# Every product of a transformer block as two 64-row halves that belong to different output tiles

## The chip, the cores and the metric

The kernel runs on one core of a Trainium2 chip. Time is device microseconds of that core for one execution, compared as medians of runs on the same chip. The engines of a core are TensorE (matrix products; in the trace PE, and PEld for its weight loads), VectorE (DVE), ScalarE (ACT), GpSimd (POOL) and SyncE (SP), whose queue issues nearly all DMAs. SBUF is the working memory with 128 partitions. PSUM, 8 banks of 2 KB a partition, is where products accumulate. [...]

## The reference

Sequence 2048, width D = 576, 32 heads of 18, feed-forward width 4608, everything float32:

```python
xn = _layernorm(x)
out = x + A(xn) + B(xn)
# A: qkv = xn @ wqkv (576 x 1728); every position attends to itself and to 7 earlier
#    ones, two apart (window 8, dilation 2); softmax over the 8; result @ wo (576 x 576)
# B: relu(xn @ w1) @ w2        (576 x 4608, 4608 x 576)
```

## The kernel before

**Tokens.** The even and the odd positions form two phases (`ph`), since a dilation of 2 never mixes them. A phase has 1024 tokens in 8 tiles of 128 (`i`), or 4 blocks of 256 (`tb`, two token tiles each).

**Precision.** Operands are split in a high part of type fp32r and a low part, so that a product of two float32 matrices is x_hi w_hi + x_lo w_hi + x_hi w_lo. D = 576 is four and a half times 128 rows. For the half, `mix` holds the 64 rows twice, their high part in partitions 0 to 63 and their low part in 64 to 127, and the weights hold the 64 rows twice. So `TERMS` (line 319) has 14 products of 128 rows: 4 + 4 with the high weights, one with `mix` and the high weights, 4 with the low weights, and one with `mix` and the low weights. That last one also computes low times low for the 64 rows, which the other rows do without.

**Slots.** Feed-forward columns are taken 128 at a time (36 groups, `c` in 12 chunks of C = 3 `f`). A slot `n` is one (ph, c, tb, f), 288 in all, `f` fastest, then `tb`; a chunk is 12 slots, a phase 144. In slot n the loop at line 765 emits, in this order and for all engines: `run_splits(n)`, the weight splits that are due; `h_mm(n + 2)`, the *first products* of a later slot (14 products of 256 columns into a bank `ph`), with their ReLU split into `hhi` (ScalarE) and `hlo` (VectorE); what is booked for the slot (`todo`: a qkv tile of 14 products of 432 columns into `pm`, transposes, wo products); `o_mm(n)`, the *second products* (two token tiles, two column cuts of 256 and 320, three terms: 12 products) into accumulators `po` that live through the three f of a token block; at f = 2 the adds of these to the residual `x` (line 613); `todo_late`; and `run_bg(margin)`, pieces of attention for VectorE as far as a count kept by the planner (`t["pe"]`, `t["dve"]`) stays within the margin, 3.0, 1.5 or 3.0 us by f. Each engine works through its own instructions strictly as emitted.

**Weights.** `split_task` queues them by step. A load is issued three tasks ahead of its split (`AHEAD`). The split (`two`, line 144) puts the high part on ScalarE and the low part on VectorE. Pools of C + 1 = 4 buffers hold w1 and w2. The step of w1 is s - 5 and that of w2 s - 3, where s is the first slot that uses it in second products (line 643).

**Attention.** A qkv unit (8 heads, 8 token tiles) starts every 26 slots from slot 7 of a phase. One tile is booked per slot, and then its attention goes to the background list.

**wo.** Each token tile's attention output is transposed by VectorE in 32-blocks and by a turn through DRAM (`wo_a`, `wo_f`), split (`wo_s`), multiplied (`wo_b`: 28 products into two `pm` banks) and added to `x`, spread over some 15 slots from 123 of a phase.

**PSUM.** Two tiles of two banks (`ps_o`), two banks for first products (`ps_h`), two for everything else (`ps_m`).

The opening (up to slot 7) is written out by hand. Between the phases, the second half of x is normed and transposed, in part by TensorE (lines 285 to 287) into `XT`.

## Time and profile before

| what | value |
|---|---|
| median of 3 runs | 1163.99 us (1163.91 to 1164.5) |
| the profiled execution, and its span | 1164.49 us, 1162.7 us |
| granted TensorE clock | 1.000 |
| TensorE busy / products | 1156.7 us / 8916 |
| VectorE busy | 822.3 us |
| ScalarE busy | 308.6 us |
| first products (`ph`) in the trace | 4018 |
| second products (`po`) | 2292 + 1146 |
| qkv products (`pm<-wq,xT`) | 896 |

How to read it: a matmul's busy time includes its run through the array, so the products overlap and a mean of 277 ns is not its price. The price is the distance between the starts of neighbours. "Idle before" of a group is how long its engine had stood still, and behind the arrow is what ended that. `ph`, `po`, `pm` are PSUM tiles; L113 is `mm`, the helper that all products go through, so that tiles and not lines tell them apart.

### The profile page before, as it was taken

Reading aid. Unit: us, or ns where it says so; the run is one execution under the profiler, and the core shown is the slowest. Engines: PE = TensorE matmul, PEld = TensorE weight load, DVE = VectorE, ACT = ScalarE, POOL = GpSimd, SP = SyncE. Lnnn points to the kernel's source line nnn. Section 1 sums busy time; section 2 is a strip of 40 time slices with the busy share of each in tenths; the row PEclk is TensorE's granted clock in tenths of the full one; section 3 lists DMA queues with packets and bytes.
Section 4 is the critical chain, followed back from the end, with each engine's and each line's share of the span. In section 5 each row is a group of like instructions: output and inputs, shape, how many; then the busy total and the mean of one; then the engine's idle time right before and its main releaser. Section 6 shows DMA issues by size and latency. Waiting matters only on the chain.

```text
span 1162.7 us, 21695 instructions
## 1 busy us (share of the span) xinstructions
PE 1156.7 (99%) x8916; PEld 1148.5 (99%) x8916; DVE 822.3 (71%) x1299; ACT 308.6 (27%) x748; POOL 44.8 (4%) x60
## 2 busy tenths in 40 slices
PE   9999999999999999999999999999999999999998
PEld 8999999999999999999999999999999999999998
DVE  7427885887687688876683288768868877887843
ACT  5322222131231221322433123222222312222210
POOL 2200100010000000000010001000100000000000
PEclk9999999999999999999999999999999999999999
DMA  5312211140321211365752113021312303113541
GB/s 184 98 32 79 69 48 54 39 112 1 94 79 32 81 39 46 96 156 112 180 164 69 43 53 95 22 81 38 87 35 61 110 1 101 46 32 95 123 100 63
DMA packets 149876, 88.66 MB, mean 76 GB/s; under 512 B 58528, under 2 KB 133536, under 8 KB 149776
## 3 DMA queue, kind: packets, MB, share of 16 engines
q1 hardware_dynamic: 146816, 78.61, 24.9%
q10 hardware_dynamic: 2960, 8.65, 2.5%
q8 instruction: 70, 1.15, 0.4%
q14 instruction: 30, 0.25, 0.1%
HBM read 67.90 MB, written 11.14 MB: 68 GB/s over the span
## 4 chain that ended last, share of the span: by engine, by line
PE 98%; SPq 1%; DMA 0%; DVE 0%; issue 0%; ACT 0%; DVEq 0%
PE ph L113 39%; PE po L113 38%; PE pm L113 20%; DMA st<-in_w 0%; PE pm L286 0%; SPq L162 0%; SPq L161 0%; DVE w2t L149 0%; SPq L157 0%; DVE x L619 0%; SPq L236 0%; PE pm L287 0%; DVE bst L250 0%; ACT w2t L145 0%; SPq L238 0%
## 5 line engine op out<-in xcount | busy, mean ns | idle before, releaser
L113 PE MATMUL ph<-xT,w1t 128*128 128x256 f32 x4018 | 504.9, 277 | 0.7 <-ACT xT L291 0.7
L113 PEld LDWEIGHTS ph<-xT,w1t 128*128 128x128 f32 x4018 | 486.7, 188 | 1.3 <-ACT xT L291 1.0
L113 PE MATMUL po<-w2t,hhi 128*128 128x256 f32 x2292 | 393.2, 293 | 0.2 <-DVE w2t L149 0.2
L113 PEld LDWEIGHTS po<-w2t,hhi 128*128 128x128 f32 x2292 | 335.4, 188 | 1.5 <-DVE w2t L149 0.4
L556 ACT ACTIVATE hhi<-ph 128x256 fp32r<-128x256 f32 x287 | 109.7, 383 | 582.3 <-PE ph L113 575.7
L113 PE MATMUL po<-w2t,hlo 128*128 128x256 f32 x1146 | 242.3, 292 | 0.0
L559 DVE SCALAR_TENSOR_TENSOR hlo<-ph,hhi 128x256 fp32r<-128x256 f32 x287 | 120.9, 421 | 164.7 <-ACT hhi L556 164.2
L113 PEld LDWEIGHTS po<-w2t,hlo 128*128 128x128 f32 x1146 | 188.9, 187 | 0.0
L113 PE MATMUL pm<-wq,xT 128*128 128x432 f32 x896 | 185.5, 358 | 0.0
L613 DVE TENSOR_TENSOR x<-po,x 128x576 f32<-128x576 f32 x190 | 143.0, 756 | 60.1 <-PE po L113 57.3
L113 PEld LDWEIGHTS pm<-wq,xT 128*128 128x128 f32 x896 | 163.8, 188 | 5.6
L421 DVE TENSOR_TENSOR pr<-qo,k 128x1152 f32<-128x1152 f32 x64 | 86.2, 1349 | 0.0
L424 DVE TENSOR_REDUCE lg<-pr 128x64 f32<-128x1152 f32 x64 | 85.1, 1343 | 0.0
L451 DVE TENSOR_TENSOR pr<-lg,v 128x1152 f32<-128x1152 f32 x64 | 84.7, 1349 | 0.0
L149 DVE TENSOR_TENSOR w2t<-st,w2t 128x576 fp32r<-128x576 f32 x72 | 55.8, 776 | 32.3 <-ACT w2t L145 32.2
L149 DVE TENSOR_TENSOR w1t<-st,w1t 128x640 fp32r<-128x640 f32 x70 | 58.8, 841 | 20.5 <-ACT w1t L145 20.4
L458 DVE TENSOR_TENSOR pr<-pr 128x288 f32<-128x288 f32 (+1 forms) x128 | 70.6, 600 | 0.0
L145 ACT ACTIVATE w2t<-st 128x576 fp32r<-128x576 f32 x72 | 49.3, 685 | 45.6 <-PE po L113 33.1
L390 ACT ACTIVATE k<-pm 128x144 f32<-128x144 f32 x64 | 18.6, 291 | 146.2 <-PE pm L113 146.2
L145 ACT ACTIVATE w1t<-st 128x640 fp32r<-128x640 f32 x72 | 52.9, 734 | 13.3 <-DMA st<-in_w 7.1
L427 POOL TENSOR_SCALAR_AFFINE_SELECT lg<-lg 1x512 f32<-1x512 f32 x8 | 9.9, 1232 | 809.7 <-DVE lg L424 705.8
L522 DVE TENSOR_TENSOR x<-pm,x 128x256 f32<-128x256 f32 (+1 forms) x32 | 13.2, 453 | 30.9 <-PE pm L113 30.9
(84 smaller groups left out, 470.8 us busy)
## 6 DMA issues: line engine op xcount, KB each, us to landing
st<-in_w SPq DMA_DIRECT2D x72, 288.0 KB, 3.1
st<-in_w SPq DMA_DIRECT2D x72, 256.0 KB, 3.2
st<-in_wqkv SPq DMA_DIRECT2D x32, 216.0 KB, 3.0
turned<-tr SPq DMA_DIRECT2D x64, 80.0 KB, 2.8
xn<-turned SPq DMA_DIRECT2D x16, 320.0 KB, 3.2
st<-in_w SPq DMA_DIRECT2D x144, 32.0 KB, 2.9
out<-x SPq DMA_DIRECT2D x15, 288.0 KB, 2.1
x<-in_x SPq DMA_DIRECT2D x14, 288.0 KB, 4.7
```

Source lines behind the costliest of these rows:

```text
L113: nc.tensor.matmul(o, l, r, start=start, stop=stop)
L145: nc.scalar.activation(hi, src, AF.Copy)
L149: nc.vector.tensor_tensor(lo, src, f32(hi), op=ALU.subtract)
L390: nc.scalar.activation(k[:, W - 1 + i, :], pq[:, 1, :], AF.Copy)
L421: nc.vector.tensor_tensor(pr[i], q, window(k, i), op=ALU.mult)
L424: nc.vector.tensor_reduce(lg[:, i], pr.pop(i).rearrange(heads, d=Dh), axis=AX.X, op=ALU.add)
L451: nc.vector.tensor_tensor(pr[i].rearrange(heads, d=Dh), e, window(v, i).rearrange(heads, d=Dh), op=ALU.mult)
L458: nc.vector.tensor_tensor(o, z[:, 0:n], z[:, n : 2 * n], op=ALU.add)
L522: nc.vector.tensor_tensor(acc, po[h], acc, op=ALU.add)
L556: nc.scalar.activation(hi, pt, AF.Relu)
L559: nc.vector.scalar_tensor_tensor(lo, pt, 0.0, f32(hi), op0=ALU.max, op1=ALU.subtract)
L613: nc.vector.tensor_tensor(acc, whole, acc, op=ALU.add)
```

## The change

Behind the opening, no product uses 128 rows any more. `mm_rows` issues two products of 64 rows each, one in partitions 0 to 63, one in 64 to 127, with different accumulators in different banks. Two output tiles are worked on together: in the first run tile A uses the lower rows and tile B the upper ones, in the second run they change places, and so each tile has both halves of the rows. Ahead of a run whose banks the other half of the rows has just written, a no-op on TensorE waits for the last product that did so.

The half tile of 64 rows is then a term of its own on either side: `LOWER` and `UPPER` have 13 pairs, `LOWER_MORE` and `UPPER_MORE` 14. For the upper side, `XT` has a tenth slice with a copy of the high part in partitions 64 to 127 (`twin`, `make_xt`, `xt_s`). Low times low of the 64 rows is not computed any more. Two tiles take 14 + 13 = 27 pairs.

First products (`h_two`): the pair of slots (g, g + 1), g = n + 2 for an even n, has its first run in slot n and its second in slot n + 1, where both ReLU splits follow. qkv (`qkv_tile`): two token tiles, first run in one slot, second in the next, then six copies. Second products (`o_two`): two token tiles, by column cut, four runs of three pairs. wo has no products of its own: its terms are appended to the second products of f = 1 in chunk 10, into the same accumulators. `ps_o` is four single banks, and the adds are four of one cut each. The steps of w1 and w2, the distance of qkv units (24) and the booking of wo's transposes are new. The `hp` pool has 3 buffers of each kind instead of 4.

```diff
+    def mm_rows(runs, behind=None):
+        if behind is not None:
+            tc.add_manual_dep(nc.tensor.nop().ins, behind.ins.name, SYNC, reason="PSUM banks change rows")
+        for pair in zip(*runs, strict=True):
+            for z, (o, l, r, start, stop, n) in zip((slice(0, 64), slice(64, P)), pair):
+                ins = nc.tensor.matmul(o, l[z], r[z], start=start, stop=stop)
+            t["pe"] += pair[0][5] / 2400.0 + 0.002
+        return ins
...
+    FULL_K = [(5 + k, k) for k in range(KT)] + [(k, k) for k in range(KT)] + [(5 + k, 5 + k) for k in range(KT)]
+    LOWER, LOWER_MORE = FULL_K + [(4, 4)], FULL_K + [(4, 4), (4, 9)]
+    UPPER, UPPER_MORE = FULL_K + [(4, 4)], FULL_K + [(4, 4), (9, 9)]
...
+        if not second:
+            for h in range(2):
+                PQ[h] = ps_m.tile([P, 3, UD], F32, name="pm")
+            PQ[2] = mm_rows((run(0, LOWER_MORE), run(1, UPPER_MORE)))
+            return
+        mm_rows((run(1, LOWER), run(0, UPPER)), PQ[2])
...
+    def h_two(g, second):
+        def run(n, terms):
+            ph, c, tb, f = slots[n]
+            w, xt = W1[ph, c, f], XT[ph, tb]
+            return [
+                (HP[n], w[:, b // 5, (b % 5) * P : (b % 5 + 1) * P], xt[:, a, :], not second and j == 0, second and j == len(terms) - 1, TBN)
+                for j, (a, b) in enumerate(terms)
+            ]
+        if not second:
+            HB["m"] = not HB["m"] and not busy_m.intersection((g - 3, g - 2, g - 1))
+            for n in (g, g + 1):
+                HP[n] = ps_m.tile([P, TBN], F32, name="pm") if HB["m"] else ps_h.tile([P, TBN], F32, name="ph")
+            HB["ins"] = mm_rows((run(g, LOWER_MORE), run(g + 1, UPPER_MORE)))
+            return
+        mm_rows((run(g + 1, LOWER), run(g, UPPER)), HB["ins"])
+        h_out(g)
+        h_out(g + 1)
...
+    def o_two(n):
+        ph, c, tb, f = slots[n]
+        hi, lo = H.pop(n)
+        w = W2[ph, c, f]
+        with_wo = c == WO_CHUNK and f == 1
+        if f == 0:
+            o_tiles(n)
...
+            z = [(l[:, cs], w[:, b, CUT[h]]) for l, b in ((hi, 0), (hi, 1), (lo, 0))]
+            if with_wo:
+                more = wo_run(ph, 2 * tb + k, h, (UPPER_MORE if upper else LOWER_MORE) if first else (UPPER if upper else LOWER), upper)
+                z = z + more
...
+        for j in range(4):
+            k, h = divmod(j, 2)
+            behind = PB[j - 2] if j > 1 else PB[3] if j == 0 and f else None
+            PB[j] = mm_rows((run(k, h, False), run(1 - k, h, True)), behind)
...
+        o_out(n, rows=True)
...
-                plan.append((HEADW[f] if first else s - 5, w1_task, ((ph, c, f), c * C + f)))
-                plan.append((HEADW[3 + f] if first else s - 3, w2_task, ((ph, c, f), c * C + f)))
+                plan.append((HEADW[f] if first else s + (-5, -4, -2)[f], w1_task, ((ph, c, f), c * C + f)))
+                plan.append((HEADW[3 + f] if first else s + (-3, -1, 0)[f], w2_task, ((ph, c, f), c * C + f)))
...
-        m = n + LAG
-        if m < len(slots):
-            h_mm(m)
+        g = n - n % 2 + LAG
+        if n < ROW0:
+            h_mm(n + LAG)
+        elif g < len(slots):
+            h_two(g, n % 2 == 1)
...
-        if n >= 0:
+        if ROW0 - 1 <= n < len(slots) - C:
+            o_two(n)
+        else:
             o_mm(n, n != HALVED)
```

The last three slots use the old `o_mm` with whole rows.

More of the change, by code (lines that the diff above doesn't have):

```diff
@@ L16 @@
 PSUM = bass.MemoryType.PSUM
+SYNC = mybir.DependencyInfo(mybir.DependencyClass.Sync, mybir.DependencyReason.DATA)
 P = 128
@@ L27 @@
 LAG = 2
+ROW0 = 8
 EPS = 1e-5
-UNIT0, UNIT_STEP, WO_AT = 7, 26, 12
+UNIT0, UNIT_STEP = 7, 24
+WO_CHUNK = 10
 XT_STEPS = (
@@ L37 @@
 )
-WO_STEPS = (0, 1, 3, 4, 6, 7, 9, 10)
+WO_STEPS = ((-5, -4), (-3, -3), (-1, -1))
 HEADW = (-9, -8, -7, -6, -5, -4)
@@ L83, in tile_body @@
     stp = pool("stp", 5)
-    hp = pool("hp", LAG + 2)
+    hp = pool("hp", LAG + 1)
     prp = pool("prp", 2)
@@ L89, in tile_body @@
     turned = pool("turned", 4, space=bass.MemoryType.DRAM)
-    ps_o = pool("ps_o", 2, space=PSUM)
+    ps_o = pool("ps_o", 4, space=PSUM)
     ps_h = pool("ps_h", 2, space=PSUM)
@@ L100, in tile_body @@
     spare = consts.tile([P, 1], F32, name="spare")
-    warm = ps_o.tile([P, 2, 512], F32, name="po")
+    warm = ps_o.tile([P, 512], F32, name="po")
     for _ in range(WARM):
-        nc.tensor.transpose(warm[:, 0, 0:P], ident, ident)
+        nc.tensor.transpose(warm[:, 0:P], ident, ident)
     x_v = x.rearrange("(p i two) d -> two i p d", i=NI, two=NPH)
@@ L278, in transpose_split @@
         if bank is ps_o:
-            po = ps_o.tile([P, 2, 512], F32, name="po")
-            pa, pb = po[:, 0, :].rearrange("p (k c) -> p k c", k=KT), po[0:DR, 1, 0:P]
+            pa = ps_o.tile([P, 512], F32, name="po").rearrange("p (k c) -> p k c", k=KT)
+            pb = ps_o.tile([P, 512], F32, name="po")[0:DR, 0:P]
         else:
@@ L312, in make_xt, with twin @@
         if h == 0:
-            XT[ph, tb] = xtp.tile([P, 9, TBN], F32R, name="xT")
+            XT[ph, tb] = xtp.tile([P, 10, TBN], F32R, name="xT")
         d = XT[ph, tb][:, :, h * P : (h + 1) * P]
         xn = XN.pop((ph, i))
-        return transpose_split(xn, d[:, 5:9, :], d[:, 4, :], d[:, 0:4, :], bank, parts)
+        steps = transpose_split(xn, d[:, 5:9, :], d[:, 4, :], d[:, 0:4, :], bank, parts)
+        if ph:
+            nc.scalar.activation(d[DR:P, 9, :], f32(d[0:DR, 4, :]), AF.Copy)
+        return steps
+    def twin(tb):
+        nc.scalar.activation(XT[0, tb][DR:P, 9, :], f32(XT[0, tb][0:DR, 4, :]), AF.Copy)
     TERMS = (
@@ L349, in xt_f @@
         if h == 0:
-            XT[ph, tb] = xtp.tile([P, 9, TBN], F32R, name="xT")
+            XT[ph, tb] = xtp.tile([P, 10, TBN], F32R, name="xT")
         z, td = f32(XT[ph, tb][:, 0:5, h * P : (h + 1) * P]), TD.pop((ph, i))
@@ L359, in xt_s @@
         d = XT[ph, tb][:, :, h * P : (h + 1) * P]
-        z = tmp.tile([P, 5, P], F32R, name="oT", bufs=1)[:, 0]
-        mix = d[:, 4, :]
+        mix, z = d[:, 4, :], d[:, 9, :]
         nc.scalar.activation(d[:, 5:9, :], f32(d[:, 0:4, :]), AF.Copy)
@@ L373, in tile_body @@
     QO, KK, VV = {}, {}, {}
+    PQ = {}
     def qkv_tile(ph, u, i):
@@ L384, in qkv_tile, with run @@
         k, v, wq = KK[ph, u], VV[ph, u], WQ[ph, u]
-        tb, h = divmod(i, 2)
+        tb, second = i // 2, i % 2 == 1
         xt = XT[ph, tb]
-        pq = ps_m.tile([P, 3, UD], F32, name="pm")
-        for j, (a, b) in enumerate(TERMS):
-            mm(pq, xt[:, a, h * P : (h + 1) * P], wq[:, b, :], j == 0, j == len(TERMS) - 1, 3 * UD)
-        nc.scalar.activation(k[:, W - 1 + i, :], pq[:, 1, :], AF.Copy)
-        nc.scalar.activation(v[:, W - 1 + i, :], pq[:, 2, :], AF.Copy)
-        nc.scalar.activation(QO[ph][:, i, u * UD : (u + 1) * UD], pq[:, 0, :], AF.Copy)
+        def run(h, terms):
+            return [
+                (PQ[h], xt[:, a, h * P : (h + 1) * P], wq[:, b, :], not second and j == 0, second and j == len(terms) - 1, 3 * UD)
+                for j, (a, b) in enumerate(terms)
[6 more added lines that the diff above has]
+        mm_rows((run(1, LOWER), run(0, UPPER)), PQ[2])
+        for h in range(2):
+            j, pq = i - 1 + h, PQ.pop(h)
+            nc.scalar.activation(k[:, W - 1 + j, :], pq[:, 1, :], AF.Copy)
+            nc.scalar.activation(v[:, W - 1 + j, :], pq[:, 2, :], AF.Copy)
+            nc.scalar.activation(QO[ph][:, j, u * UD : (u + 1) * UD], pq[:, 0, :], AF.Copy)
         if i == NI - 1:
@@ L505, in wo_s, with wo_run @@
         z = f32(r)
-        d = tmp.tile([P, 5, P], F32R, name="oT", bufs=1)
+        if i == 0:
+            OH[ph] = kp.tile([P, 2, 5, P], F32R, name="k")
+        d = OH[ph][:, i % 2]
         nc.scalar.activation(d, z, AF.Copy)
         nc.vector.tensor_tensor(r[:, 0:KT], z[:, 0:KT], f32(d[:, 0:KT]), op=ALU.subtract)
-        nc.vector.tensor_tensor(d[DR:P, KT], z[DR:P, KT], f32(d[DR:P, KT]), op=ALU.subtract)
+        nc.vector.tensor_tensor(r[DR:P, KT], z[DR:P, KT], f32(d[DR:P, KT]), op=ALU.subtract)
         dve(512)
         dve(128)
-        OT[ph, i] = [r[:, k] for k in range(KT)] + [d[:, KT]] + [d[:, k] for k in range(KT)]
-    def wo_b(ph, i):
-        d, w = OT.pop((ph, i)), WO[ph]
-        po = [ps_m.tile([P, c.stop - c.start], F32, name="pm") for c in CUT]
-        for j, (a, b) in enumerate(TERMS):
-            for h, c in enumerate(CUT):
-                mm(po[h], d[a], w[b][:, c], j == 0, j == len(TERMS) - 1, D2)
-        for h, c in enumerate(CUT):
-            acc = X[ph, i][:, c]
-            nc.vector.tensor_tensor(acc, po[h], acc, op=ALU.add)
-            dve(D2)
-    left = {(ph, i): 2 for ph in range(NPH) for i in range(NI)}
-    def done(ph, i):
-        left[ph, i] -= 1
-        if left[ph, i] == 0:
-            nc.sync.dma_start(o_v[ph, i], X[ph, i])
+        OT[ph, i] = r, d
+    OH = {}
+    def wo_run(ph, i, h, terms, upper):
+        r, d = OT[ph, i]
+        row = [r[:, j] for j in range(KT)] + [r[:, KT] if upper else d[:, KT]] + [d[:, j] for j in range(KT + 1)]
+        return [(row[a], WO[ph][b][:, CUT[h]]) for a, b in terms]
     slots = [(ph, c, tb, f) for ph in range(NPH) for c in range(NCH) for tb in range(NTB) for f in range(C)]
@@ L570, in h_mm, with o_tiles, run @@
         h_out(n)
-    def half(po, h):
-        if isinstance(po, list):
-            return po[h]
-        return po[:, 1, 0 : D - 256] if h else po[:, 0, 256:512]
+    HB = {"m": False}
+    def h_two(g, second):
+        def run(n, terms):
+            ph, c, tb, f = slots[n]
+            w, xt = W1[ph, c, f], XT[ph, tb]
+            return [
+                (HP[n], w[:, b // 5, (b % 5) * P : (b % 5 + 1) * P], xt[:, a, :], not second and j == 0, second and j == len(terms) - 1, TBN)
+                for j, (a, b) in enumerate(terms)
+            ]
+        if not second:
[7 more added lines that the diff above has]
+        h_out(g + 1)
+    def o_tiles(n):
+        for h, c in enumerate(CUT):
+            for k in range(2):
+                PO[k, h] = ps_o.tile([P, 512], F32, name="po")[:, 0 : c.stop - c.start]
+    def o_two(n):
[5 more added lines that the diff above has]
+            o_tiles(n)
+        def run(k, h, upper):
+            cs, first = slice(k * P, (k + 1) * P), k == upper
+            z = [(l[:, cs], w[:, b, CUT[h]]) for l, b in ((hi, 0), (hi, 1), (lo, 0))]
+            if with_wo:
+                more = wo_run(ph, 2 * tb + k, h, (UPPER_MORE if upper else LOWER_MORE) if first else (UPPER if upper else LOWER), upper)
+                z = z + more
+            return [
+                (PO[k, h], l, r, f == 0 and first and j == 0, f == C - 1 and not first and j == len(z) - 1, CUT[h].stop - CUT[h].start)
+                for j, (l, r) in enumerate(z)
+            ]
+        for j in range(4):
+            k, h = divmod(j, 2)
+            behind = PB[j - 2] if j > 1 else PB[3] if j == 0 and f else None
+            PB[j] = mm_rows((run(k, h, False), run(1 - k, h, True)), behind)
+        if with_wo:
+            for k in range(2):
+                OT.pop((ph, 2 * tb + k))
+        o_out(n, rows=True)
+    PB = [None] * 4
     def o_mm(n, out=True, which=range(2)):
@@ L581, in o_mm @@
         end = n == len(slots) - 1
+        if f == 0 and 0 in which:
+            o_tiles(n)
         for k in which:
-            if f == 0 and n == len(slots) - C:
-                if k:
-                    PO[k] = [ps_m.tile([P, c.stop - c.start], F32, name="pm") for c in CUT]
-                else:
-                    PO[k] = [ps_o.tile([P, 2, 512], F32, name="po")[:, 0, 0 : c.stop - c.start] for c in CUT]
-            elif f == 0:
-                PO[k] = ps_o.tile([P, 2, 512], F32, name="po")
             cs = slice(k * P, (k + 1) * P)
@@ L595, in o_mm @@
                 mm(
-                    half(PO[k], h), l[:, cs], w[:, b, CUT[h]],
+                    PO[k, h], l[:, cs], w[:, b, CUT[h]],
                     f == 0 and j == 0, f == C - 1 and j == 2, D2,
@@ L602, in o_mm, with o_out @@
             o_out(n, which)
-    def o_out(n, which=range(2)):
+    def o_out(n, which=range(2), rows=False):
         ph, c, tb, f = slots[n]
@@ L607, in o_out @@
             return
-        for k in which:
-            i = 2 * tb + k
-            acc = X[ph, i]
-            if n < len(slots) - 1:
-                whole = PO[k].rearrange("p b c -> p (b c)")[:, 256 : 256 + D]
-                nc.vector.tensor_tensor(acc, whole, acc, op=ALU.add)
-                dve(D)
-                if c == NCH - 1:
-                    done(ph, i)
-                continue
-            for h, c in reversed(list(enumerate(CUT))):
-                nc.vector.tensor_tensor(acc[:, c], half(PO[k], h), acc[:, c], op=ALU.add)
-                if k:
-                    (nc.scalar if h else nc.sync).dma_start(o_v[ph, i][:, c], acc[:, c])
-            if k == 0:
-                done(ph, i)
+        end = n == len(slots) - 1
+        order = [(k, h) for k in which for h in range(2)]
+        if rows:
+            order.sort(key=lambda z: z[1])
+        elif end:
+            order.sort(key=lambda z: (z[0], -z[1]))
+        for k, h in order:
+            i = 2 * tb + k
+            acc, cols = X[ph, i], CUT[h]
+            nc.vector.tensor_tensor(acc[:, cols], PO[k, h], acc[:, cols], op=ALU.add)
+            dve(cols.stop - cols.start)
+            if end and k:
+                (nc.scalar if h else nc.sync).dma_start(o_v[ph, i][:, cols], acc[:, cols])
+            elif c == NCH - 1 and (k, h) in (order[-1], order[-2 if rows else 1]):
+                nc.sync.dma_start(o_v[ph, i], acc)
     todo = {}
@@ L636, in tile_body @@
     plan = []
+    busy_m = set()
     for ph in range(NPH):
@@ L649, in tile_body @@
                 at(s + i, qkv_tile, ph, u, i)
+                busy_m.add(s + i)
             late(s + NI + 1, attention, ph, u)
-        s = b + UNIT0 + NU * UNIT_STEP + WO_AT
-        plan.append((s - 8, wo_tasks, (ph,)))
+        plan.append((b + WO_CHUNK * SPC - 6, wo_tasks, (ph,)))
         for i in range(NI):
-            z = s + WO_STEPS[i]
-            late(z, wo_a, ph, i)
-            at(z + 1, wo_f, ph, i)
-            late(z + 3, wo_s, ph, i)
-            at(z + 4, wo_b, ph, i)
-            at(z + 4, done, ph, i)
+            z = b + WO_CHUNK * SPC + C * (i // 2) + 1
+            out_at, in_at, parts_at = (z + k[i % 2] for k in WO_STEPS)
+            late(out_at, wo_a, ph, i)
+            late(in_at, wo_f, ph, i)
+            at(parts_at, wo_s, ph, i)
         if ph + 1 < NPH:
@@ L663, in tile_body @@
                 if i >= len(XT_STEPS):
-                    z = e + 3 + 2 * i
+                    z = e + 3 + 2 * i - (i == NI - 1)
                     at(z - 6, load_x, ph + 1, i)
@@ L668, in tile_body @@
                     at(z + 1, make_xt, ph + 1, i)
+                    busy_m.add(z + 1)
                     continue
@@ L762, in tile_body @@
         (late if k else at)(z, {"stats": stats, "norm": norm, "xt": make_xt}[op], 0, *a)
+    for tb in range(NTB):
+        late((4, 4, 6, 7)[tb], twin, tb)
     M = (3.0, 1.5, 3.0)
-    AT_WO = range(UNIT0 + NU * UNIT_STEP + WO_AT, UNIT0 + NU * UNIT_STEP + WO_AT + 12)
+    AT_WO = range(WO_CHUNK * SPC - 4, (WO_CHUNK + 1) * SPC)
     for n in range(FIRST, len(slots)):
         run_splits(n)
-        m = n + LAG
-        if m < len(slots):
-            h_mm(m)
+        g = n - n % 2 + LAG
[3 more added lines that the diff above has]
+            h_two(g, n % 2 == 1)
         for f, a in todo.pop(n, []):
             f(*a)
-        if n >= 0:
+        if ROW0 - 1 <= n < len(slots) - C:
+            o_two(n)
+        else:
             o_mm(n, n != HALVED)
```

## The prediction

> **What bounds the kernel now.** I read the engine totals first, then the chain that ended last, then TensorE's waits, and last two stretches in order of time.

> ```profile
> PE 1156.7 (99%) x8916; PEld 1148.5 (99%) x8916; DVE 822.3 (71%) x1299; ACT 308.6 (27%) x748; POOL 44.8 (4%) x60
> ...
> PE 98%; SPq 1%; DMA 0%; DVE 0%; issue 0%; ACT 0%; DVEq 0%
> PE ph L113 39%; PE po L113 38%; PE pm L113 20%; DMA st<-in_w 0%; PE pm L286 0%; SPq L162 0%; SPq L161 0%; DVE w2t L149 0%; SPq L157 0%; DVE x L619 0%; SPq L236 0%; PE pm L287 0%; DVE bst L250 0%; ACT w2t L145 0%; SPq L238 0%
> ```

> The first line is busy time, the other two are the chain by engine and by line. 98% of it is TensorE, so each product more or less counts, and each wait that TensorE does not have now is added in full.

> TensorE's waits, all of them (total, times, longest):

> ```profile
> PE po L104 <- POOL mhalf L99: 1.3, 1, 1.3
> PE ph L113 <- ACT xT L291: 0.7, 1, 0.7
> PE po L113 <- DVE w2t L149: 0.2, 1, 0.2
> ```

> 2.2 us in all, and all before 30 us. Now one slot in order of time (start, length, engine, line, tiles, count), its TensorE, VectorE and ScalarE:

> ```profile
> 103.31 0.68 PE L113 MATMUL po<-w2t,hhi 128*128 128x256 f32 x4
> 103.83 0.42 PE L113 MATMUL po<-w2t,hlo 128*128 128x256 f32 x2
> 104.09 0.68 PE L113 MATMUL po<-w2t,hhi 128*128 128x256 f32 x4
> 104.61 0.42 PE L113 MATMUL po<-w2t,hlo 128*128 128x256 f32 x2
> 104.87 1.76 PE L113 MATMUL ph<-xT,w1t 128*128 128x256 f32 x14
> 106.47 0.68 PE L113 MATMUL po<-w2t,hhi 128*128 128x256 f32 x4
> ```
> ```profile
> 103.93 0.42 DVE L559 SCALAR_TENSOR_TENSOR hlo<-ph,hhi 128x256 fp32r<-128x256 f32 x1 [1.56 <-ACT hhi L556]
> 104.29 1.54 DVE L613 TENSOR_TENSOR x<-po,x 128x576 f32<-128x576 f32 x2
> 105.75 1.35 DVE L421 TENSOR_TENSOR pr<-qo,k 128x1152 f32<-128x1152 f32 x1
> 107.01 0.75 DVE L149 TENSOR_TENSOR w2t<-st,w2t 128x576 fp32r<-128x576 f32 x1
> 107.68 0.82 DVE L149 TENSOR_TENSOR w1t<-st,w1t 128x640 fp32r<-128x640 f32 x1
> ```
> ```profile
> 103.79 0.68 ACT L145 ACTIVATE w2t<-st 128x576 fp32r<-128x576 f32 x1
> 104.37 0.74 ACT L145 ACTIVATE w1t<-st 128x640 fp32r<-128x640 f32 x1
> ```

> The reader is to see two things. First, prices: 14 first products from 104.87 to 106.47 are 0.114 us each, 12 second ones from 103.31 to 104.87 are 0.130 us. Second, VectorE's order behind a slot with f = 2, as the code emits it: the adds of the finished accumulators, one piece of attention, and only then the low parts of the weights due in the next slot. The low part of w1 is ready at 107.68 + 0.82 = 108.50, which is 3.63 us after the next slot began (104.87). Nothing waits for it now, because w1 is split (s - 5) three slots before its first product. A qkv tile, and a restart after a wait:

> ```profile
> 40.29 2.90 PE L113 MATMUL pm<-wq,xT 128*128 128x432 f32 x14
> 43.03 0.70 PE L113 MATMUL po<-w2t,hhi 128*128 128x256 f32 x4
> ...
> 8.17 0.60 ACT L291 ACTIVATE xT<-po 128x512 fp32r<-128x512 f32 x1
> 8.82 0.61 PE L113 MATMUL ph<-xT,w1t 128*128 128x256 f32 x3 [0.69 <-ACT xT L291]
> ```

> So 2.74 / 14 = 0.196 us for a product of 432 columns; and 0.05 us from a producer's end (8.77) to TensorE's start. That product takes 0.384 us (longest of the ph row) instead of 0.276: its weights load for 0.11 first. A restart costs 0.16.

> **The change, part by part.** The sum is made on the profiled execution, 1164.49 us (span 1162.7 and 1.8 around it); the median is 0.5 below it.

> *Products saved.* Two tiles need 27 pairs where they took 28 products. First products from slot 10 on: 139 pairs of slots, 139 x 0.114 = 15.8. qkv: 32 pairs of tiles x 0.196 = 6.3. wo: 8 pairs of tiles x 2 column cuts x 0.130 = 2.1. The second products stay 12 pairs a slot. Sum -24.2 us, if a pair takes what one full product takes.

> *Price of a pair.* The trace has no 64-row product. Above: two loads of weights behind one another. After the restart at 8.82 the second load starts 0.11 later with nothing else in its way, so a pair whose two loads queue takes at least 0.22. Below: the best rate per column in the trace is the first products', 0.114 / 256 = 0.445 ns; at this rate the 3768 pairs of 288 columns give 2 ns each and the 864 of 432 columns 4 ns, 11 us together. A gain beyond that is not excluded. I take the full product's time, the nearest row: the same columns run through the same 128 rows, half of them for each accumulator.

> *The weights' new due times.* This decides. w1 moves from s - 5 to s - 5, s - 4, s - 2 for f = 0, 1, 2. The pair of slots (cs + 2, cs + 3), where cs is a chunk's first slot, is begun at the top of slot cs, and its f = 2 weight is split with step (cs + 2) - 2 = cs, so in the same slot, right ahead of it, and behind the w2 of f = 1, which is due at cs too. Slot cs - 1 has f = 2, so VectorE stands exactly as in the stretch shown: adds, one piece of attention, w2t, w1t. It gets worse by 0.30, since four adds of 256 and 320 columns (425 and 481 ns in the rows of L522, 1.81 together) replace two of 756, and by 0.38, since both slots' hlo now lie just ahead of the adds, and the first two accumulators end one product run (3 x 0.140) before the slot does: adds start 0.20 before the slot's end instead of 0.58. Ready at 3.63 + 0.68 = 4.31 us into the slot. TensorE asks for the low part at the ninth pair, 8 x 0.114 = 0.91 us in. Wait 3.40, and 0.16 for the restart: 3.56 us. Without a piece of attention (1.26 from 105.75 to 107.01) it is 2.30. There are 23 chunk boundaries; in the trace now an attention operation follows the adds at 18 of them. 18 x 3.56 + 5 x 2.30 = 75.6 us. ScalarE's high parts come at about 0.9 and lie inside this wait. Weight f = 1 (split at cs - 3, asked for one slot of 3.1 us later) comes 0.4 late where attention runs and no qkv phase lies between, some 12 times: 5 us with restarts. The third w2 (split in its own slot) is late only against a 1.5 us margin of attention that the wait before it has used up: nothing, else 0.6 x 23 = 14.

> *Waits on changing rows.* The no-op ahead of a second phase waits for a run that ended at least twelve pairs ago: hidden. In the second products it waits for the run before the last: 0.303 for the last product (the 302 ns row), 0.05 and 0.11 make 0.46, against 0.14 + 3 x 0.120 = 0.50 of pairs still queued. Hidden by 0.04, so the cover is thin; if a no-op takes what an event instruction on TensorE's queue takes (51 ns), 0.01 x 278 = 3 us. I take 3. Without cover at two runs a slot, 556 x 0.1 = 56. Behind this wait all of the next phase is queued.

> *Switching between whole and half rows.* Four sets of transposes in the middle, and both ends: about ten switches. Nothing in the trace switches; between nothing and a full run-out (0.276 + 0.16 = 0.44) that is 0 to 4.4, I take 2. [...]

> *Beside TensorE.* VectorE: 32 adds of wo go (14.5 us), 190 adds grow by 0.15 (28): 836 of some 1220, not the bound. The banks of the next tile pair: adds end 1.6 us into the slot, asked for at 1.60 and 1.96: hidden. hi and lo have 3.1 us instead of 6.3 from the phase's end to their use and need 0.9 to 1.6. Six copies of qkv (1.75) have 3.1. wo's transposes keep their 64 + 16 DMAs on SP's queue and their distance; a fetch waits there for the tile buffer of the slot just done, with weight loads behind it, which are three tasks ahead. POOL gets nothing.

> Sum: 1164.5 - 24.2 + 75.6 + 5 + 3 + 2 = 1225.9; on the median's scale 1225.

> **Rivals.** (A) *Pairs run quicker than full products*, faster than before. One half's weights would load while the other half's columns stream. For it: second products of 256 columns start 0.120 apart and first ones 0.114, so part of the time is no streaming. Against it: the rows by columns above give 11 us, not 62. It decides from 61 us / 8385 pairs = 7.3 ns a pair; at 9 ns the time is 1150.
> (B) *Pairs cost a few ns more.* A load starts 3 to 4 ns behind the product before it, and a product 2 ns behind a load when nothing blocks: one more load and product in line is 5 ns a pair, 8385 x 5 = 42, 1267 us. Against: a second half need not be in the first one's way. [...]
> (C) *Loads queue*: 0.22 a pair. 8385 x 0.22 = 1845, plus 51 for what stays whole, plus the waits: about 1960 us. Against: the halves use different rows.
> (D) *The row-change waits are not covered*: 56 instead of 3, 1278 us.

> **How the numbers follow.** Forecast 0.48, A 0.20 (0.16 of it faster, 0.02 within, 0.02 slower), B 0.15, C 0.09, D 0.08. The forecast's own range is 1201 (no attention at any boundary: 23 x 2.30 = 53) to 1242. Leaving out C and the lower part of A: 1150 to 1300. Under 0.2%, 2.3 us, a measurement of this kernel tells nothing from no change. Faster 0.16, same 0.02, slower 0.82.

> **What would show it.** In the new trace TensorE's waits should name DVE w1t, some 23 times, 2.3 to 3.6 us each, ahead of first products, one chunk (12 slots) apart. Pairs of 256 columns should start 0.114 apart; 27 pairs for two slots; second products 0.130. No wait on the banks po. The forecast is wrong if those waits are absent, or if pair spacing differs from the full product's by over 3 ns (25 us).

## The result, and the profile after

The changed kernel takes 1311.07 us (1308.74 to 1312.54) against 1164.03 us beside it: 1.126 times as long, interval 1.1241 to 1.128. The profiled execution took 1312.54 us, 148.0 more than the one of before. Slower was forecast, by 61 us; the time lies 11 us above the upper end of the range, 1300. Engine totals, granted clock and the chain by engine, from the page of the changed kernel:

```profile
PE 1203.6 (92%) x17114; PEld 1182.5 (90%) x17114; DVE 804.0 (61%) x1457; ACT 287.1 (22%) x756; POOL 44.5 (3%) x60
...
PEclk9999989999998999999989999898999989999999
...
PE 75%; DVE 17%; issue 2%; DMA 2%; SPq 1%; ACT 1%; POOL 0%; DVEq 0%; POOLq 0%; ACTq 0%
```

The chain that was 98% TensorE is 75% TensorE and 17% VectorE, so something on VectorE is now waited for. And the clock row has eights among its nines, where the page of before has nines throughout: the mean is 0.963, it was 1.000. The waits of TensorE (total, times, longest):

```profile
PE ph L126 <- DVE w1t L163: 43.0, 18, 4.9
PE pm L126 <- DVE w1t L163: 29.1, 14, 2.3
PE ph L126 <- DVE hlo L591: 13.3, 7, 2.1
PE pm L126 <- ACT w1t L159: 8.0, 14, 2.3
PE ph L126 <- ACT w1t L159: 5.4, 1, 5.4
```

85.5 us are for w1 weights (72.1 low parts from VectorE in 32 waits, 13.4 high parts from ScalarE), 14.5 for the low half of the ReLU output (`hlo`, the two waits of a second product, 1.2, included). One chunk boundary in order of time (start, length, engine, line, tiles, form, count, and in brackets the idle time before and its releaser; the form 64*128 64x256 is weights of 64 rows by 128 columns with 256 columns run through them), TensorE and then VectorE:

```profile
117.50 1.21 PE L126 MATMUL pm<-xT,w1t 64*128 64x256 f32 x16 [0.35 <-ACT w1t L159]
121.02 1.37 PE L126 MATMUL pm<-xT,w1t 64*128 64x256 f32 x12 [2.31 <-DVE w1t L163]
122.19 0.63 PE L126 MATMUL po<-w2t,hhi 64*128 64x256 f32 x4
...
124.94 1.22 PE L126 MATMUL pm<-xT,w1t 64*128 64x256 f32 x18
```
```profile
116.74 1.55 DVE L699 TENSOR_TENSOR x<-po,x 128x256 f32<-128x256 f32 x4
118.21 1.35 DVE L461 TENSOR_TENSOR pr<-qo,k 128x1152 f32<-128x1152 f32 x1
119.47 0.76 DVE L163 TENSOR_TENSOR w2t<-st,w2t 128x576 fp32r<-128x576 f32 x1
120.14 0.82 DVE L163 TENSOR_TENSOR w1t<-st,w1t 128x640 fp32r<-128x640 f32 x1
```

This is the order that the prediction worked out: adds, one piece of attention, w2, w1. The slot begins at 116.94; the low part ends at 120.96, 4.02 us into it (4.31 was worked out), and TensorE goes on at 121.02. What the prediction did not see stands behind the wait. The second products at 122.19 take until 124.94, 2.75 us, where 1.593 is the median of such a slot. Two stretches of the changed kernel, ahead of this wait and behind it (us, then busy time and count of PE, PEld, DVE, ACT and POOL, then granted clock, DMA share, GB/s):

```profile
113.00:117.00 4.00, 4.00 (x66) 3.88 (x62) 1.37 (x4) 1.41 (x4) 0.00 (x0) 1.00 0.25 73
121.40:124.70 3.30, 3.30 (x33) 3.30 (x32) 0.82 (x1) 0.00 (x0) 0.00 (x0) 0.50 0.51 137
```

Busy from end to end in both, and with nearly the same mix of shapes, TensorE starts 16.5 products a microsecond in the first and 10 in the second, where the granted clock is 0.50. The trace has 20 such stretches, 95.6 us in all, and in 16.8 of these TensorE stood still. An estimate of what the other 78.8 cost is 33 us by the slot shown (1 - 1.593 / 2.75 = 0.42 of the time) and 39 at one half. (Some of the expectations below say 48 us of halved clock: that is one half of the 95.6, standing still included.)

Last, a spacing where nothing waits and the clock is full:

```profile
113.86 1.69 PE L126 MATMUL ph<-xT,w1t 64*128 64x256 f32 x26
115.34 0.44 PE L126 MATMUL po<-w2t,hhi 64*128 64x256 f32 x4
```

13 pairs from 113.86 to 115.34, 0.114 each: a pair of halves costs what one full product cost. The single records say more than these merged rows: most halves of this run start 50 ns apart and the next pair 64 ns behind, in other runs it is 3 to 4 and 110, and the sum is the same.

The account of the 148.0 us: -24.2 for the products saved, +85.5 waits for w1, +14.5 waits for `hlo`, +33 to 39 clock. That leaves 33 to 39, of which some 18 is spacing: where nothing waits and the clock is full, first products start 116.3 ns apart on the mean instead of 114.1 (3753 pairs, 8 us), and a slot of second products takes 1.593 us instead of 1.559 (medians, 278 slots, 9.5 us). Some 9 are restarts, an estimate: the 56 waits for w1 and `hlo` at the prediction's 0.16 each. The last 6 to 12 are not placed.

### The profile page after: what moved, and what is told of

Read it like the earlier page. It is cut to its first block, busy times and chain, and to the rows that moved or that the text cites. A ratio compares the mean times of both kernels' runs of the same rounds, so it can differ in the third digit from the quotient of the medians.

```text
span 1310.7 us, 38255 instructions
## 1 busy us (share of the span) xinstructions
PE 1203.6 (92%) x17114; PEld 1182.5 (90%) x17114; DVE 804.0 (61%) x1457; ACT 287.1 (22%) x756; POOL 44.5 (3%) x60
## 4 chain that ended last, share of the span: by engine, by line
PE 75%; DVE 17%; issue 2%; DMA 2%; SPq 1%; ACT 1%; POOL 0%; DVEq 0%; POOLq 0%; ACTq 0%
PE po L126 33%; PE pm L126 23%; PE ph L126 18%; DVE x L699 5%; DVE w1t L163 2%; DVE w2t L163 2%; DVE pr L491 2%; DVE lg L464 2%; DVE pr L498 1%; DMA st<-in_w 1%; DVE hlo L591 1%; DVE pr L461 1%; PE po L116 0%; DVE lg L486 0%; SPq L353 0%
## 5 line engine op out<-in xcount | busy, mean ns | idle before, releaser
L126 PE MATMUL po<-w2t,hhi 64*128 64x256 f32 (+1 forms) x4448 | 467.0, 298 | 0.3 <-DVE w2t L163 0.3
L126 PEld LDWEIGHTS po<-w2t,hhi 64*128 64x128 f32 x4448 | 381.6, 190 | 2.4 <-issue 0.8
L126 PE MATMUL ph<-xT,w1t 64*128 64x256 f32 x4698 | 317.8, 280 | 61.6 <-DVE w1t L163 43.0
L126 PEld LDWEIGHTS ph<-xT,w1t 64*128 64x128 f32 x4698 | 301.4, 188 | 68.5 <-DVE w1t L163 46.7
L126 PE MATMUL po<-w2t,hlo 64*128 64x256 f32 (+1 forms) x2224 | 354.0, 297 | 1.2 <-DVE hlo L591 1.2
L126 PEld LDWEIGHTS po<-w2t,hlo 64*128 64x128 f32 x2224 | 235.6, 190 | 1.6 <-DVE hlo L591 1.6
L126 PE MATMUL pm<-xT,w1t 64*128 64x256 f32 x2808 | 193.2, 285 | 37.2 <-DVE w1t L163 29.1
L126 PEld LDWEIGHTS pm<-xT,w1t 64*128 64x128 f32 x2808 | 181.7, 192 | 43.6 <-DVE w1t L163 31.9
L126 PE MATMUL pm<-wq,xT 64*128 64x432 f32 x1728 | 189.3, 366 | 0.0
L126 PEld LDWEIGHTS pm<-wq,xT 64*128 64x128 f32 x1728 | 170.7, 194 | 3.2
```

The costliest lines, as they stand in the source:

```text
L126: ins = nc.tensor.matmul(o, l[z], r[z], start=start, stop=stop)
```

## The experiments

The theory: the due times of the weights (w1 of f = 2 split in the slot that uses it) cost the waits, and the waits cost the clock. The rivals: the waits come from the halved rows themselves or from their banks, or the clock falls because of the new shape of the products and not because of standing still. Kernels named `early_...` all carry the edit of the first one.

**The due times alone undone** (`early_due`):

```diff
-  s + (-5, -4, -2)[f], w1_task     s + (-3, -1, 0)[f], w2_task
+  s + (-5, -5, -4)[f], w1_task     s + (-3, -2, -1)[f], w2_task
```

> The changed kernel with w1 due at s - 5, s - 5, s - 4 and w2 at s - 3, s - 2, s - 1 for f = 0, 1, 2, so that each split lies at least one slot ahead of its first product. Theory 1 (the weights' due times put VectorE's low parts behind the adds and a piece of attention, and the clock is halved after the longer ones of these waits): the 86 us of waits for w1t and the 48 us of halved clock go, granted clock 1.00, about 1178 us. Theory 2 (the pairs themselves are slow, or the waits come with working on two tiles at once): over 1250 us.

Measured: 1185.41 us, 1.0186 (1.0162 to 1.021), 7 above what was expected. So 126 of the 147 us go with the two tuples of numbers. TensorE's waits, this kernel:

```profile
PE ph L126 <- DVE hlo L591: 9.9, 8, 3.1
PE po L126 <- ACT k L549: 3.6, 3, 2.4
```

(`k` at L549 is the high part of an operand of wo.) No w1 stands at the top any more (0.2 us are left of those waits), the waits for `hlo` stay, and the mean clock is 0.996. The new shape of the products is all there, so it is not what lowers the clock.

**The due times alone, on the kernel before** (`before_late_due`): the reverse edit, with all products whole.

```diff
-  s - 5, w1_task                   s - 3, w2_task
+  s + (-5, -4, -2)[f], w1_task     s + (-3, -1, 0)[f], w2_task
```

> The kernel before, whole products and all, with only the changed kernel's due times of w1 and w2. Theory 1: TensorE waits for w1t at the chunk boundaries, 18 x 2.9 + 5 x 1.6 = 60 us, and loses some 25 to 45 us to a halved clock behind them: 1240 to 1270 us, without any 64-row product. Theory 2: 1164 us, nothing waits.

Measured: 1275.67 us, 1.0954 (1.0935 to 1.0972). TensorE's waits:

```profile
PE ph L113 <- DVE w1t L149: 54.8, 23, 4.2
PE ph L113 <- ACT w1t L145: 10.6, 9, 3.4
```

65.4 us at 23 boundaries, and 15 stretches at half clock (78.5 us, 12.6 of them standing still, so some 28 to 33 lost), on whole 128-row products. The time is 6 us above what was expected. Waits and clock need neither halves nor pairs.

**No attention ahead of a chunk boundary** (`no_attention_there`), on the changed kernel:

```diff
-        run_bg(1.5 if n % SPP in AT_WO else M[slots[n][3]])
+        if n % SPC != SPC - 1:
+            run_bg(1.5 if n % SPP in AT_WO else M[slots[n][3]])
```

> The changed kernel, but the last slot of each chunk starts no piece of attention (the other slots do). Theory 1 (VectorE's order): each wait for w1t at a boundary gets shorter by the pieces that stood ahead, 1.3 us, or 3.2 us where a qkv tile lies in that slot; w1t waits 72 us -> about 40, halved clock 48 us -> 15 to 25, about 1255 us. Theory 2: the waits stay, 1311 us.

Measured: 1255.96 us, 1.0789 (1.0773 to 1.0805). TensorE's waits:

```profile
PE ph L126 <- DVE w1t L163: 24.2, 19, 1.7
PE pm L126 <- DVE w1t L163: 14.5, 14, 1.6
```

The waits for low parts fall from 72.1 to 38.7 us, so the attention ahead of the split made 33 of them; the longest falls from 4.9 to 1.7. The half clock falls from 95.6 to 34.1 us. 55 us less for 33 us of waits: most of the other 22 is the clock.

**The wait filled with products** (`filled_wait`). Ahead of each chunk's first run, 20 more pairs run into the same banks, which the real run then overwrites; they are no part of the computation. They keep TensorE busy for 20 x 0.114 = 2.3 us where it would stand still:

```diff
+            if g % SPC == LAG:
+                ph, c, tb, f = slots[g + 1]
+                for _ in range(20):
+                    for z, m in ((slice(0, 64), g), (slice(64, P), g + 1)):
+                        nc.tensor.matmul(HP[m], W1[ph, c, f][z, 0, 0:P], XT[ph, tb][z, 5, :], start=True, stop=True)
```

> The changed kernel with 20 pairs of products (2.3 us) that nobody reads ahead of the first run of each chunk, where TensorE waits for the weight; their bank is cleared by the run that follows. The wait for w1t is shorter by what the products take, so the work in the way stays as long. Theory 1 (standing still is what halves the clock): halved clock 48 us -> under 15, total 1311 - 35 to 48, 1263 to 1276 us. Rival (the clock is halved for 64-row products or for the load, not for standing still): clock as before and 1311 us or more.

Measured: 1288.59 us, 1.1056 (1.1025 to 1.1088). The same boundary as above, TensorE in order of time:

```profile
117.30 2.48 PE L625 MATMUL pm<-xT,w1t 64*128 64x256 f32 x40
119.58 1.10 PE L126 MATMUL pm<-xT,w1t 64*128 64x256 f32 x16
121.36 0.97 PE L126 MATMUL pm<-xT,w1t 64*128 64x256 f32 x12 [0.68 <-DVE w1t L163]
122.17 0.39 PE L126 MATMUL po<-w2t,hhi 64*128 64x256 f32 x4
```

TensorE goes on at 121.36 instead of 121.02, but its next 12 products now take 0.81 us instead of 1.17, and the granted clock from 121.40 to 124.70 is 1.00 instead of 0.50. Over the kernel 53.6 us of useless products replace 51 us of waiting, and the time still falls by 22, because the half clock falls from 95.6 to 27.3 us. That settles the cause of the clock: standing still, not the shape. The halved clock came out as expected (at one half the 27.3 us cost 14, under 15). The total lies 13 us above the near end, because what could be saved was set too high: the clock had cost 33 to 39, not 48, since TensorE stood still in part of those stretches, and the products added take 3 us more than the waits they replace. Of the 8 stretches that remain only three stand behind waits for w1 (two of 2.5 us, one of 1.7); four follow waits of 2.1 us for `hlo`, which nothing fills, and one a wait of 1.3 us for the adds to `x`.

**One number alone put back** (`one_due_time`): w1 of f = 2 split one slot earlier.

```diff
-  s + (-5, -4, -2)[f], w1_task
+  s + (-5, -4, -3)[f], w1_task
```

> The changed kernel with one number changed: w1 of f = 2 due at s - 3 instead of s - 2, one slot earlier. If this one weight is what the long waits at chunk boundaries are for, they go with the halved clock: of 86 us of waits for w1t some 12 to 20 stay (f = 1, 1.2 each where attention runs), hlo's 14 stay, halved clock under 8: 1200 to 1220 us. If the other due times carry a good part, over 1240 us.

Measured: 1210.69 us, 1.0397 (1.0381 to 1.0413). One digit is worth 100 us. TensorE's waits for w1 that are left are mainly those of f = 1:

```profile
PE ph L126 <- DVE w1t L163: 10.2, 10, 1.0
```

Ten waits of 1.0 us, where the prediction had some 12 of 0.4.

**What the halves themselves cost.** Three kernels, each against `early_due`. In `early_uncovered_rows` the no-op that waits for the other half's last product has no run of products between:

```diff
-            k, h = divmod(j, 2)
-            behind = PB[j - 2] if j > 1 else PB[3] if j == 0 and f else None
+            h, k = divmod(j, 2)
+            behind = PB[j - 1] if j % 2 else PB[3] if j == 0 and f else None
```

> The kernel with early due times, its four runs of second products in another order: the two runs that share banks and change rows follow one another, so that the no-op ahead of the second waits for a product just issued, twice a slot, 556 times. If the wait is what the restart row says (0.30 of the product, 0.05 to the engine, 0.11 of loading), less the 0.12 to 0.15 by which the next product would have started anyway, it costs about 0.33 each, 556 x 0.33 = 184 us: about 1370 us. If the wait in the order of the changed kernel is not covered either, nothing changes: 1185 us.

Measured: 1358.95 us, 1.1666 (1.1647 to 1.1686). Two neighbouring runs of this kernel:

```profile
303.79 0.40 PE L126 MATMUL po<-w2t,hhi 64*128 64x256 f32 x4
...
304.36 0.50 PE L126 MATMUL po<-w2t,hhi 64*128 64x256 f32 x4
...
304.82 0.46 PE L126 MATMUL po<-w2t,hhi 64*128 64x320 f32 x4
```

The run that a change of rows follows takes 0.57 us, the next run of the same columns 0.46, for three pairs that take 0.35 when nothing waits: 0.33 for the change. A whole slot takes 2.25 instead of 1.59, which is 0.33 for each of its two. By the totals, 173.5 us for 556 such changes, it is 0.31. So the order in the changed kernel, with one run between, does cover the wait: 0.04 us of calculated cover held.

In `early_whole_second` the second products are whole again, and TensorE changes between halves and whole rows twice a slot, some 510 times:

```diff
-        if ROW0 - 1 <= n < len(slots) - C:
+        if ROW0 - 1 <= n < len(slots) - C and (n < 9 or slots[n][1] == WO_CHUNK):
```

> The kernel with early due times (1185 us), but second products as whole 128-row products as in the kernel before, except in the wo chunk; first products and qkv stay 64-row pairs. TensorE then changes between half and whole rows twice a slot, about 510 times. If a change costs nothing, second products fall from 1.594 to 1.560 us a slot and the time is about 1176 us. If each change runs the array out (0.28 + 0.16 us, the prediction's upper end), 1176 + 225 = 1400 us; at the restart's 0.16 us alone 1258 us. The prediction took 0.2 a change.

Measured: 1264.89 us, 1.0864 (1.0848 to 1.088). Against `early_due` 79.5 us more; if the whole second products gave back 278 x 0.034 = 9.5, that is 89 / 510 = 0.175 us a change. This is too little, since `early_due` stood still for some 20 us and this kernel for 6. The rows show a change directly:

```profile
301.35 1.80 PE L126 MATMUL ph<-xT,w1t 64*128 64x256 f32 x26
303.08 0.79 PE L116 MATMUL po<-w2t,hhi 128*128 128x256 f32 x4
...
304.83 1.42 PE L126 MATMUL pm<-xT,w1t 64*128 64x256 f32 x20
```

The 13 pairs take 1.73 us (1.49 without a change), the 12 whole products 1.75 (1.56): 0.43 for the two changes, about 0.2 each. The medians over all slots, 1.79 for second products and 1.70 for 13 pairs, give the same 0.2. The ten or so changes in the kernel are 2 us, which is what the prediction took. The 0.44 that I made of a full run-out is twice what is measured.

In `early_even_cut` the column cuts of the second products are 288 and 288 instead of 256 and 320:

```diff
-    CUT = (slice(0, 256), slice(256, D))
+    CUT = (slice(0, D2), slice(D2, D))
```

> The kernel with early due times, columns of the second products and of wo cut 288 and 288 instead of 256 and 320. In the changed kernel a pair of 256 columns takes 0.117 us and one of 320 takes 0.149 (0.120 and 0.140 as whole products). If the time goes with the columns, a pair of 288 is 0.133 and nothing moves: 1185 us within 2. If the halves get in each other's way above some number of columns between 256 and 320, a pair of 288 may be at 0.120 to 0.125 and the time 1158 to 1172.

Measured: 1185.77 us, 1.0184 (1.0169 to 1.0199), as `early_due`. A pair of 288 columns takes 0.133, the mean of 0.117 (256) and 0.147 to 0.149 (320). Whole products of 320 columns took 0.140. The loss is in the second products with either cut. It is not the pairing alone: in `early_whole_second` a whole product of 320 columns also takes 0.147 (median), and the whole ones of 256 columns 0.117. What makes a wide product take 7 to 9 ns more in these kernels stays open.

**Is there a version that gains?** Four kernels take away the waits that `early_due` has left. `early_calm` lets less attention run ahead and issues loads one task earlier:

```diff
-    AHEAD = 3
-    M = (3.0, 1.5, 3.0)
+    AHEAD = 4
+    M = (2.0, 1.5, 1.5)
```

> The kernel with early due times, its attention margins 2.0, 1.5, 1.5 instead of 3.0, 1.5, 3.0 us and weights loaded 4 tasks ahead instead of 3. What is left of TensorE's waits there is VectorE late with hlo (9.9 us in 8 waits), a weight load late at wo, and 3.4 us of halved clock. If VectorE's attention pieces ahead of hlo are the cause, some 8 to 15 us go: 1170 to 1177 us. If not, 1185 us.

Measured: 1173.98 us, 1.0086 (1.0071 to 1.0101). The waits for `hlo` fall from 9.9 to 1.1 us, those for wo's operand (`k`, L549) rise to 6.8. `early_margin_ahead3` holds attention back only in slots with a qkv tile, and moves wo's transposes earlier:

```diff
-WO_STEPS = ((-5, -4), (-3, -3), (-1, -1))
+WO_STEPS = ((-6, -5), (-4, -3), (-1, -1))
-        run_bg(1.5 if n % SPP in AT_WO else M[slots[n][3]])
+        run_bg(1.5 if n % SPP in AT_WO or n in busy_m else M[slots[n][3]])
```

> Early due times, attention margin 1.5 us in slots with a qkv tile and 3.0, 1.5, 3.0 elsewhere, wo's turns through DRAM one slot earlier and the first tile's fetch one slot earlier, weights loaded 3 tasks ahead. Of the 1174 us of the calm kernel, some 7 us were a wait for wo's fetched tiles, queued on SP behind weight loads, and 3.4 us the halved clock behind it. If both go and hlo stays in time: 1163 to 1167 us. What the pairs save (24) would then stand against some 10 us that second products take longer in pairs, 6 in first ones, and 4 at the two ends.

Measured: 1174.18 us, 1.0084 (1.007 to 1.0098), above what I expected: 3.0 us of waits for the adds to `x` and 3.2 for `hlo` are left. `early_margin_ahead4` is the same with `AHEAD = 4`:

> The same with weights loaded 4 tasks ahead: fewer weight loads late at wo, but more of them ahead of wo's fetches on SP's queue. 1163 to 1170 us.

Measured: 1170.24 us, 1.0047 (1.0035 to 1.006), at the far end. `early_wo_early` is that kernel with the wo weights split four slots earlier:

```diff
-        plan.append((b + WO_CHUNK * SPC - 6, wo_tasks, (ph,)))
+        plan.append((b + WO_CHUNK * SPC - 10, wo_tasks, (ph,)))
```

> The kernel with early due times, margins and loads 4 ahead (1170 us), its wo weights split four slots earlier, away from the slot ahead of the wo chunk, where VectorE's adds came late to the banks of the next tiles (3.4 us, and 1.7 us of halved clock in one phase). 1165 to 1168 us if that was the cause, else 1170.

Measured: 1164.11 us (1162.6 to 1164.88), 0.9998 (0.9989 to 1.0007): the same as before, and 1 us below what was expected. Its engine totals, and TensorE in order of time around one run of first products:

```profile
PE 1155.1 (99%) x17114; PEld 1146.4 (99%) x17114; DVE 802.3 (69%) x1457; ACT 287.6 (25%) x756; POOL 46.1 (4%) x60
```
```profile
112.39 0.39 PE L126 MATMUL po<-w2t,hhi 64*128 64x256 f32 x4
...
113.99 1.77 PE L126 MATMUL pm<-xT,w1t 64*128 64x256 f32 x28
115.59 0.39 PE L126 MATMUL po<-w2t,hhi 64*128 64x256 f32 x4
```

TensorE is busy 99% of the span, its clock is 1.000, its waits add up to some 4 us, and still nothing is gained over the kernel before. Second products take 1.60 here (112.39 to 113.99) and the 14 pairs 1.60. Over the kernel, from start to start of neighbouring groups and without the last three slots, first products take 451.9 us where 444.3 was to be, and second products with wo 519.3 where 503.1 was to be: 7.6 + 16.2 of the 24.2 saved. 1.8 of the 16.2 are waits, and 0.9 more goes into the transposes between the phases. qkv takes 168.6 where 168.9 was to be, so there the saving is kept in full. Elsewhere slightly slower pairs use it up.

## Why the prediction was right and wrong

- **The waits for w1**: right in place, count and mechanism, and near in total: 75.6 + 5, restarts included, against 85.5 of standing still (75.2 at the 23 boundaries, 10.3 in ten waits for f = 1) and, as an estimate, 7 of restarts on top (47 waits at 0.16). The mechanism is shown: one number undone takes 100 us away, and the same numbers on the kernel before bring 112 us. That the sum comes so near is in part luck, since single sizes were off both ways. At ten boundaries with one or two pieces of attention TensorE stood still for 2.4 to 2.7 us; at the one shown it went on 3.17 us late (121.02 against 116.94 + 0.91), where 3.40 to 3.56 was worked out. "One piece of attention" was too few at six boundaries behind a slot with a qkv tile: there three pieces ran ahead of the split, because by the code the planner's count for TensorE is further on by then, and TensorE stood still for 4.9 us. And f = 1 was 1.0 late, not 0.4. One of the six, TensorE and VectorE:

```profile
181.52 1.65 PE L126 MATMUL ph<-xT,w1t 64*128 64x256 f32 x12 [4.89 <-DVE w1t L163]
```
```profile
176.78 2.62 DVE L491 TENSOR_TENSOR pr<-lg,v 128x1152 f32<-128x1152 f32 x2
179.31 0.75 DVE L498 TENSOR_TENSOR pr<-pr 128x576 f32<-128x576 f32 x1
```

- **What the sum left out**: the granted clock. The step that failed is "Wait 3.40, and 0.16 for the restart": a wait was priced at its length and a restart. 20 stretches at half clock behind the waits cost another 33 to 39 us. This alone takes the sum from 1225 to some 1260, and it was not among the rivals either; with the next two points (14.5 and 18 us) and some 14 more for w1 and all restarts it carried the time over 1300. The profile of before could not show it, since its longest wait is 1.3 us.
- **"hi and lo have 3.1 us instead of 6.3 ... and need 0.9 to 1.6"**, taken as hidden: wrong, 14.5 us in 9 waits. With attention running ahead on VectorE the low half came up to 2.1 us late. Holding attention back took these waits to 0.8 in `early_wo_early`.
- **The price of a pair**: right within a run of first products, 113.5 ns for 114; over the kernel 2.2 ns too low for first products (8 us) and 34 ns too low for a slot of second ones (9.5 us). This is the term mis-sized, and it is what leaves the repaired version without a gain.
- **Rival A** (pairs quicker): false, no spacing is below the whole product's beyond 3 ns (0.117 us against 0.120 for second products of 256 columns). **B** (5 ns for each further half): not seen as a mechanism, though pairs did cost 2 to 3 ns more over the kernel, about half of its price. The second half starts 3 to 50 ns late, and the next pair is not pushed back by that: in `early_wo_early` runs of first products whose halves start 3 to 6 ns apart have a period of 115.0 ns, those with 45 to 60 have 113.9. **C** (loads queue, 0.22): false; its sum, 1845 + 51 and the waits, is 1977, not 1960. **D** (uncovered changes of rows): false here, and priced at 0.31 to 0.33 us each, three times the 0.1 that I had given it.
- **Changes between whole and half rows**: 2 us taken, and about 2 by measurement (ten at the 0.2 of `early_whole_second`).
- **The banks**: "No wait on the banks po" held in the changed kernel (`early_due` has two, 3.0 us).

## What to carry to other kernels

When a change moves a weight's preparation toward its use, write down the order of the preparing engine's queue at that point, the background pieces too, and compare the end with the product that asks; it gave the sum of these waits to within some 15%, and single ones to within 1.5 us. Then price a TensorE wait of over 2 us at its length plus about 1.5 us of half-speed work behind it, an estimate from these traces (0.42 to 0.5 of a stretch of 3.413 us, the shorter of the two lengths of half clock in the changed kernel). A saving of 2% in products needs the spacing of the new shape known to 1%, and that is measured by one kernel in which nothing waits.

## What the runs showed of the hardware

**Two 64-row loads did not queue.** The loads of a pair's halves lie beside one another: at 114.44 of the changed kernel they take 184 ns each and start 50 ns apart, at 91.03 there and at 114.46 of `early_wo_early` 3 ns apart. A pair of 256 columns had the period of one 128-row product in first products: 13 pairs from 113.86 to 115.34, 0.114 us each.

**A change of a bank's rows**, with the no-op that waits for it, cost 0.31 to 0.33 us where nothing lies between (`early_uncovered_rows`), and nothing that the rows show where a run of three pairs does (changed kernel: 1.593 us a slot instead of 2.25). A change between whole rows and halves cost about 0.2 us (`early_whole_second`: 13 pairs in 1.73 us instead of 1.49, 12 whole products in 1.75 instead of 1.56).
